# Recurrent attention and gMLP on one core: V sets, last-stage order, flag read and first weight load rearranged

## The chip, the core and the metric

The kernel runs on one core of a Trainium2 chip. TensorE (PE) multiplies, ScalarE (ACT) and VectorE (DVE) evacuate the accumulator banks (PSUM) and do the softmax and normalization, GpSimd (POOL) helps with small copies, and SyncE (SP) issues most DMAs. The metric is the device time of one execution in microseconds; a version is timed in several runs, and the median counts.

## The reference

Input: x of 2048 rows of 512, bf16. First a layernorm and an attention that is recurrent in its memory, 32 heads of 128, over 64 segments of 32 rows; then a gated MLP whose gate mixes all 2048 rows.

```python
def _A_ref(x, mem0, Wq, Wk, Wv, Wo, seg_len):     # x is the layernorm of the input
    mask = (idx[:, None] < M) | (idx[:, None] >= idx[None, :])   # M = 8 memory rows
    mem = mem0
    for s in range(n_seg):                          # 64
        xs = x[:, s * seg_len:(s + 1) * seg_len, :]
        h = jnp.concatenate([mem, xs], axis=1)      # 40 rows
        q, k, v = h Wq, h Wk, h Wv                  # per head
        p = softmax(where(mask, q k^T * scale, -1e9))
        o = einsum('bhte,hed->btd', p v, Wo)
        mem = o[:, :M, :]                           # feeds the next segment
        outs.append(o[:, M:, :])

def _B_ref(x, w_in, w_sp, b_sp, w_out):
    z = gelu(x w_in)                                # 512 -> 1792
    z1, z2 = z[..., :896], layernorm(z[..., 896:])
    g = einsum('ts,bsf->btf', w_sp, z2) + b_sp      # mixes all 2048 rows
    return einsum('bsf,fd->bsd', z1 * g, w_out)

h  = x + _A_ref(layernorm(x), ...)
h2 = h + _B_ref(layernorm(h), ...)
```

## The kernel before

All instructions come from lists that are written in order, one list for each engine; each engine runs its list in that order. An operation names what it reads and writes by tokens, and the emitter turns these into semaphore waits. Nothing reorders at run time, so where a matmul stands in the code of a segment is where PE runs it.

The work has four stages. In the start (to about 41.6 us) x, its normalization and the weights are loaded and the projections of the first chunk of 16 segments are made: `qkx_full` (L449) projects, for Q and K, "extra" rows of a chunk, eight of every segment's 32, head by head; `load_w(0, hq)` loads Wq in four pieces of eight heads, on the SP and ACT queues at once. Then come 64 segments one after the other, since each reads the memory rows that the one before made. A segment is QK (L539), scores (L590, L611) with the softmax on ACT, DVE and POOL, V (L645), PV (L670, and L676 for the extra rows), Wo (L708), and the memory rows (L735). PE would wait for the softmax and for the evacuation of PV; so PE gets filler matmuls there that later work needs: 16 matmuls from the list `gx` (L426, projections of the next chunk's extra rows), sets of four V matmuls for extra rows from the queue `gv` (L476), the output projection of the extra rows (`WoX_mm`, L764, with F matmuls L746 that collect a block's rows), and early gMLP projections (`zp_mm`, L836, 448 wide). `gv.pour(n)` takes up to n atoms of the queue, each with four matmuls, and stops at an atom that completes a bank, whose evacuation is then due. There are three places for it in a segment: ahead of PV, between PV and Wo, and behind Wo ("late"). With j4 = s % 4 and rb = s // 4, the pour ahead of PV happens where `rb == 0 or j4 < 3`; one between PV and Wo only if that one gave nothing.

PV writes four column groups c of 32 partitions; for each half b the four L676 matmuls come last, in the order c = 0, 1, 2, 3. Then ACT copies the groups c = 0 (each half apart) and c = 1 to `cT` (L694) and DVE c = 2 and c = 3 (L696). Wo reads the groups in the order 0, 2, 1, 3.

The last stage makes z2 (`z2_mm`, L1224: two groups of four matmuls of 448 columns a block) for the blocks from 10 to 15, while those from 0 to 9 were prepared within the segments; it normalizes z2 (`z2_norm`, `z2_apply` on DVE), makes z1 (`z1_group`, L1257, four matmuls of 512 columns) and mixes: out of each block of `order` five mix matmuls (L1264) go into five banks, with a lag of four blocks; the rest of the mixing and the output product (L1359) follow. Block 15 of the attention output is finished here too: an F group, 32 WoX matmuls, a scatter (L787), two adds on DVE, and its normalized rows, with those of block 14, are transposed by PE (L1333). The mixing weights come in slices by `load_wT` (L992) on SP.

A flag says whether the fast path may be used for these inputs; a small reduction and `check_flag` make it in mid-mixing. At the end each engine waits for it, reads it into a register (`reg_load`, L2073), SP waits for all DMAs, and each branches to the general path if it is set.

Of the kernel before, what the change touches and what calls it, by code (L numbers as in the profile page):

```python
# [169 lines left out]
def fast_path(nc, st, keep, A_x, A_mem0, A_Wq, A_Wk, A_Wv, A_Wo, A_seg_len, B_w_in, B_w_sp, B_b_sp, B_w_out, out):  # L170
# [8 lines left out]
    RB = S // 128  # L179
# [125 lines left out]
    def load_w(mi, hq, queues=("sp",)):  # L305
# [12 lines left out]
    for hq in range(4):  # L318
        load_w(0, hq, ("sp", "act"))
# [123 lines left out]
    def qkx_full(ck, i, bank):  # L443
        mi, h0 = i // 8, 4 * (i % 8)
        ws = (w_q, w_k)[mi]
        for hh in range(4):
            h = h0 + hh
            for dc in range(DC):
                pe(lambda e, h=h, dc=dc, hh=hh: e.matmul(ps[:, bank, hh * 128:(hh + 1) * 128], lhsT=ws[:, dc, h * DH:(h + 1) * DH],  # L449
                                                         rhs=hTe[:, ck, dc, :], start=(dc == 0), stop=(dc == DC - 1)),  # L450
                   reads=[("hTe", ck), ("W", mi, h // 8) if mi or dc < 2 else ("W", mi, h // 8, 1)], writes=[PB(bank)])
# [212 lines left out]
    def PV_half(s, b):  # L664
# [9 lines left out]
        for c in PVO[0]:  # L674
# [67 lines left out]
    def F_group(rb, bank, alone=False):  # L742
        sel, tok = (F2_sb, "F2") if alone else (F_sb, "F")
        for j in range(4):
            i = (4 * rb + j) % 8
            pe(lambda e, i=i, j=j: e.matmul(ps[32 * j:32 * j + 32, bank, :], lhsT=sel[:, :], rhs=part[:, i, :], start=True, stop=alone,  # L746
                                            tile_position=(0, 32 * j)),
               reads=[("part", i, 0), ("part", i, 1), tok] + ([("pm", rb % 2, g) for g in range(4)] if alone else []), writes=[PB(bank)])
# [11 lines left out]
    def WoX_mm(rb, qr, bgs=range(8)):  # L760
        for bg in bgs:
# [3 lines left out]
                                                           start=(i < 4), stop=(i >= H - 4), tile_position=(0, 32 * g)),  # L765
# [17 lines left out]

    def WoX_scatter(rb, bank, alone=False):
        for c in range(4):
            q = slice(32 * c, 32 * c + 32)
            pe(lambda e, q=q, c=c: e.matmul(ps[q, bank, :], lhsT=Sc[:, q], rhs=partx[:], start=alone, stop=True, tile_position=(0, 32 * c)),  # L787
               reads=["partx", "Sc"], writes=[PB(bank)])
# [217 lines left out]

    def wxp(rb, j4):
# [12 lines left out]
    for s in range(NSEG):  # L1020
# [104 lines left out]
        pv = gv.pour(1) if rb == 0 or j4 < 3 else []  # L1125
# [52 lines left out]
        if turn or (not pv and (s < 2 or s == 3 * CK + 1)):  # L1178
            late += [lambda f=f: f("act") for f in gv.pour(1)]
# [32 lines left out]
    def check_flag(bank):  # L1212
        pe(lambda e: e.matmul(ps[0:1, bank, 0:1], lhsT=okb[:, 0:1], rhs=onesrc[:, 0:1], start=True, stop=True),
# [20 lines left out]
    order = [NZP] + list(range(NZP)) + list(range(NZP + 1, RB))  # L1234
# [70 lines left out]
    sp(lambda e: e.dma_start(bsp_b, bass.AP(B_b_sp.tensor, B_b_sp.offset, [[0, 128], [1, S]])), writes=["bsp"], after=[lastK])  # L1305
    for i, rb in enumerate(order):
# [847 lines left out]
```

## Time and profile before

| what | value |
|---|---|
| runs | 843.51, 844.49 and 846.04 us; median 844.49 |
| profiled execution | 843.96 us, of which the span from the first to the last instruction is 842.1 |
| granted TensorE clock | 0.998 |
| busy: PE, ACT, DVE, POOL | 828.8, 513.3, 483.1, 145.5 us |
| attention ends, first mix, last matmul | 678.04, 693.27, about 837.65 us |

In the profile, a line number names the place in the code; a helper that makes many operations has one line. The chain of waits lists in order of time what ended last at each step: start, duration, engine and line. PEld is the weight load of a matmul, which overlaps the matmuls. A table by window gives, for each stretch of time, the busy time of PE, PEld, DVE, ACT and POOL with counts, then the granted clock, the busy share of the DMA engines and GB/s. A q behind an engine's name (SPq, ACTq) is its sequencer.

### The profile page before, as it was taken

The page shows a single profiled execution, that of the slowest core. Times are in us where ns is not written, and L with a number is a line of the kernel's source. Part 1 is how long each engine was busy: PE and PEld are TensorE (multiplying, and loading weights), DVE is VectorE, ACT ScalarE, POOL GpSimd, SP SyncE. Part 2 cuts the span into 40 slices and gives each one's busy share as a digit, 9 for nine tenths or more (in the row PEclk, how much of TensorE's full clock was granted, in tenths as well). Part 3 has the DMA queues.
Part 4 walks back from the last instruction along what each step waited for, and adds up shares of the span by engine and source line. Part 5 has one row for each costly group of instructions (what it writes and reads, how often), then busy time and mean ns, then how long its engine had stood idle before and what let it go on. Part 6 is the DMA issues. An engine that isn't in the chain of part 4 may idle for free.

```text
span 842.1 us, 48381 instructions
## 1 busy us (share of the span) xinstructions
PE 828.8 (98%) x21968; PEld 479.7 (57%) x21974; DVE 483.1 (57%) x1224; ACT 513.3 (61%) x1547; POOL 145.5 (17%) x413
## 2 busy tenths in 40 slices
PE   8999999999999999999999999999999999999997
PEld 8665555555565555555655556555556544444443
DVE  4546565656565666665656656565556576554343
ACT  3466777777777777777777777777667676300000
POOL 5212111111211111121112111211111123100000
PEclk9999999999999999999999999999999999999999
DMA  9982222221222222221212222433334289022101
GB/s 329 386 228 75 73 61 60 60 60 56 63 73 55 67 56 65 68 70 54 74 48 66 59 56 70 102 90 89 77 83 89 65 278 287 1 101 92 53 12 47
DMA packets 106180, 80.01 MB, mean 95 GB/s; under 512 B 48552, under 2 KB 95536, under 8 KB 105968
## 3 DMA queue, kind: packets, MB, share of 16 engines
q1 hardware_dynamic: 104048, 74.03, 30.0%
q8 instruction: 174, 2.85, 1.5%
q10 hardware_dynamic: 1648, 2.49, 0.9%
q14 instruction: 38, 0.31, 0.1%
q0 software_dynamic: 272, 0.33, 0.1%
HBM read 43.72 MB, written 22.87 MB: 79 GB/s over the span
## 4 chain that ended last, share of the span: by engine, by line
PE 95%; DMA 2%; ACT 1%; SPq 1%; issue 1%; DVE 1%; ACTq 0%; POOL 0%; DVEq 0%
PE f_ps L539 27%; PE f_ps L708 14%; PE f_ps L645 13%; PE f_ps L1264 12%; PE f_ps L426 4%; PE f_ps L764 4%; PE f_ps L476 3%; PE f_ps L1359 3%; PE f_ps L670 3%; PE f_ps L449 2%; PE f_ps L836 2%; PE f_ps L1257 2%; PE f_ps L590 2%; PE f_ps L611 1%; PE f_ps L1224 1%; DMA f_arena<-in_A_Wq_dram 1%
## 5 line engine op out<-in xcount | busy, mean ns | idle before, releaser
L539 PE MATMUL f_ps<-f_arena,f_hT 128*32 128x512 bf16 (+1 forms) x5120 | 241.7, 337 | 0.3
L539 PEld LDWEIGHTS f_ps<-f_arena,f_hT 128*32 128x32 bf16 x5120 | 117.5, 96 | 99.3 <-ACT f_hT L738 33.8
L550 ACT ACTIVATE f_Tst<-f_ps 128x512 bf16<-128x512 f32 (+2 forms) x320 | 146.8, 511 | 35.1 <-PE f_ps L539 34.3
L645 PE MATMUL f_ps<-f_arena,f_hT 128*32 128x512 bf16 x2048 | 139.1, 379 | 0.0
L708 PE MATMUL f_ps<-f_arena,f_cT 128*32 128x256 bf16 x4096 | 131.0, 273 | 0.4 <-ACT f_cT L694 0.2
L635 POOL TENSOR_TENSOR f_E_sb<-f_R_sb,f_E_sb 128x64 bf16<-128x64 f32 x128 | 47.4, 370 | 407.5 <-ACT f_R_sb L627 406.9
L708 PEld LDWEIGHTS f_ps<-f_arena,f_cT 128*32 128x32 bf16 x4096 | 97.9, 96 | 24.4 <-ACT f_cT L694 8.5
L558 DVE STREAM_TRANSPOSE f_QT<-f_Tst 128x256 uint32<-128x256 uint32 x128 | 57.1, 446 | 84.3 <-ACT f_Tst L550 79.7
L657 DVE TENSOR_SCALAR f_V_sb<-f_ps 128x512 bf16<-128x512 f32 (+1 forms) x128 | 71.4, 558 | 54.2 <-PE f_ps L645 54.2
L1264 PE MATMUL f_ps<-f_arena 128*128 128x512 bf16 x448 | 100.6, 379 | 1.0 <-DMA f_arena<-wT_d 1.0
L1264 PEld LDWEIGHTS f_ps<-f_arena 128*128 128x128 bf16 x448 | 43.7, 98 | 53.5 <-DMA f_arena<-wT_d 1.1
L696 DVE TENSOR_SCALAR f_cT<-f_ps 128x256 bf16<-128x256 f32 x128 | 48.4, 420 | 40.6 <-PE f_ps L676 40.6
L604 ACT ACTIVATE f_E_sb<-f_ps 128x224 bf16<-128x224 f32 x128 | 45.4, 355 | 39.0 <-PE f_ps L616 38.0
L694 ACT ACTIVATE f_cT<-f_ps 128x160 bf16<-128x160 f32 (+1 forms) x192 | 51.5, 328 | 25.4 <-PE f_ps L676 25.1
L558 DVE STREAM_TRANSPOSE f_KT<-f_Tst 128x256 uint32<-128x256 uint32 (+2 forms) x192 | 60.8, 342 | 5.7 <-ACT f_Tst L550 3.0
L727 ACT ACTIVATE f_part<-f_ps 128x256 bf16<-128x256 f32 x128 | 49.2, 384 | 19.9 <-PE f_ps L708 14.3
L645 PEld LDWEIGHTS f_ps<-f_arena,f_hT 128*32 128x32 bf16 x2048 | 46.4, 95 | 20.1 <-issue 0.3
L738 ACT ACTIVATE f_hT<-f_ps 128x16 bf16<-128x16 f32 x126 | 23.2, 184 | 46.6 <-PE f_ps L735 46.6
L1270 DVE TENSOR_TENSOR f_arena<-f_ps,f_arena 128x512 f32<-128x512 f32 x28 | 19.3, 690 | 52.7 <-PE f_ps L1264 52.7
L576 DVE CAST f_ps<-f_mask 128x224 f32<-128x224 bf16 x80 | 29.8, 373 | 28.6 <-ACT f_hT L406 25.7
L627 ACT ACTIVATE f_R_sb<-f_R_sb 128x160 f32<-128x160 f32 x128 | 43.1, 337 | 4.4 <-ACT f_Vs L488 0.4
L426 PE MATMUL f_ps<-f_arena,f_hTe 128*32 128x512 bf16 x640 | 41.5, 379 | 0.0
(131 smaller groups left out, 1154.7 us busy)
## 6 DMA issues: line engine op xcount, KB each, us to landing
wT_d<-f_wst SPq DMA_DIRECT2D x64, 128.0 KB, 1.7
f_arena<-wT_d SPq DMA_DIRECT2D x32, 256.0 KB
f_arena<-in_A_Wv_dram SPq DMA_DIRECT2D x4, 1024.0 KB
f_arena<-in_A_Wk_dram SPq DMA_DIRECT2D x4, 1024.0 KB
f_arena<-in_A_Wo_dram SPq DMA_DIRECT2D x4, 1024.0 KB
f_Vx<-vext_d SPq DMA_DIRECT2D x62, 64.0 KB
vext_d<-f_Vs SPq DMA_DIRECT2D x22, 128.0 KB, 2.9
zp_d<-f_Vs SPq DMA_DIRECT2D x20, 112.0 KB
```

The costliest lines, as they stand in the source:

```text
L426: pe(lambda e, c=c, rhs=rhs: e.matmul(ps[32 * c:32 * c + 32, bank, :], lhsT=hTe[:, ck, dc, 32 * sg:32 * sg + 32], rhs=rhs, start=(dc == 0) ...
L539: pe(lambda e, dc=dc, c=c, rhs=rhs: e.matmul(ps[32 * c:32 * c + 32, bank, 0:32 * nh], lhsT=hT[:, sl, dc, :], rhs=rhs, start=(dc == 0), sto ...
L550: act(lambda e: e.activation(out=st_.rearrange("p (hp i r) -> p hp i r", i=32, r=2), in_=ps[:, bank, 0:64 * np_].rearrange("p (hp r i) -> ...
L558: dve(lambda e: e.transpose(out=dst, in_=src), reads=tok, writes=[(nm, b, k) for k in halves(b, p0, np_)])
L635: pool(lambda e: e.tensor_tensor(out=ev, in0=rv, in1=ev, op=ALU.mult), reads=[("R", b), ("Ex", b)], writes=[("Ex", b)])
L645: pe(lambda e, dc=dc, c=c, c0=c0: e.matmul(ps[32 * c:32 * c + 32, bank, 0:w], lhsT=hT[:, sl, dc, :], rhs=w_v[:, dc, c0:c0 + w], start=(dc ...
L657: dve(lambda e: e.tensor_scalar(out=dst, in0=src, scalar1=VSC, scalar2=None, op0=ALU.mult), reads=[PB(bank)], writes=tok)
L694: act(lambda e: e.activation(out=dst, in_=src, func=ACT.Copy, scale=UNSC), reads=[PB(bank)], writes=tok)
L696: dve(lambda e: e.tensor_scalar(out=dst, in0=src, scalar1=UNSC, scalar2=None, op0=ALU.mult), reads=[PB(bank)], writes=tok)
L708: pe(lambda e, h=h, g=g, i=i, b=b, c=c: e.matmul(ps[32 * g:32 * g + 32, bank, 0:d1 - d0], lhsT=cTh[:, i, 8:40], rhs=w_o[:, h, d0:d1], star ...
L727: act(lambda e: e.activation(out=part[:, s % 8, d0:d1], in_=ps[:, bank, 0:d1 - d0], func=ACT.Copy), reads=[PB(bank)], writes=[("part", s % ...
L1264: pe(lambda e: e.matmul(ps[:, bank, 0:TB], lhsT=z2[:, sc, fb * 128:(fb + 1) * 128], rhs=wTb[tb % 2][:, :, sc, :], start=first, stop=last), ...
```

## The change

Five edits. (1) The first piece of Wq is split: heads 0 to 3 alone, then heads 4 to 7, each on both queues; the first projection group waits for the first part alone. (2) The L676 matmuls of PV's second half come in the order c = 2, 1, 3, 0. (3) The V set ahead of PV is poured by `v_ahead`: in the first and the last block of four segments, and else only at j4 = 0 and 1 (1 and 2 in block 12); what is not poured there comes between PV and Wo, and the late pour also happens in segment 2. (4) In the last stage block 15's attention output is finished first; the order of z2 blocks is a list in which 11 comes third and 12 and 13 come later; block 15's scatter is one matmul with 128 columns; blocks 14 and 15 are stored and read back by a transposing DMA instead of by PE; the second slice set of mixing weights, w_out and h are loaded behind that. (5) The flag is read at the start of the third of four parts of mixing, where SP also waits for all DMAs issued until then; at the end SP waits for those issued since.

```diff
-    def load_w(mi, hq, queues=("sp",)):
+    def load_w(mi, hq, queues=("sp",), u=None):
         parts = len(queues)
         n = DC // parts
         wd, ws = ((A_Wq, w_q), (A_Wk, w_k), (A_Wv, w_v))[mi]
         wr = wd.rearrange("(dc p) h e -> p dc (h e)", p=128)
-        cols = slice(hq * 8 * DH, (hq + 1) * 8 * DH)
+        cols = slice(hq * 8 * DH, (hq + 1) * 8 * DH) if u is None else slice(4 * u * DH, 4 * (u + 1) * DH)
         for k in range(parts):
-            tok = ("W", mi, hq) if k == 0 else ("W", mi, hq, k)
+            tok = ("Wh", k) if u == 0 else ("W", mi, hq) if k == 0 else ("W", mi, hq, k)
             em.add(queues[k], lambda e, k=k: e.dma_start(ws[:, k * n:(k + 1) * n, cols], wr[:, k * n:(k + 1) * n, cols]), dma=True, writes=[tok])
             em.mark_const(tok)
 
     load_xe(0, 0)
     load_xe(1, 1, "act")
     for hq in range(4):
-        load_w(0, hq, ("sp", "act"))
+        for u in (None,) if hq else (0, 1):
+            load_w(0, hq, ("sp", "act"), u)
         if hq == 1:
             act(lambda e: e.preload_act_table_set("natural_log_exp_and_others"))
     load_x(0, 4)
...
-                   reads=[("hTe", ck), ("W", mi, h // 8) if mi or dc < 2 else ("W", mi, h // 8, 1)], writes=[PB(bank)])
+                   reads=[("hTe", ck), ("Wh", dc // 2) if i == 0 else ("W", mi, h // 8) if mi or dc < 2 else ("W", mi, h // 8, 1)], writes=[PB(bank)])
...
-        for c in PVO[0]:
+        for c in (PVO[0], (2, 1, 3, 0))[b]:
...
         for bg in bgs:
             b, g = bg // 4, bg % 4
             h = 16 * b + 4 * qr + g
             pe(lambda e, h=h, g=g, i=8 * qr + bg: e.matmul(ps[32 * g:32 * g + 32, WXB, :], lhsT=cTx[:, rb % 2, i, :], rhs=w_o[:, h, :],
-                                                           start=(i < 4), stop=(i >= H - 4), tile_position=(0, 32 * g)),
+                                                           start=(i // 8 == first and i % 8 < 4), stop=(i // 8 == last and i % 8 >= 4), tile_position=(0, 32 * g)),
                reads=[("cTx", rb % 2, qr), ("Wo", h // 8)], writes=[PB(WXB)])
     def WoX_range(rb, i0, i1):
...
+    def v_ahead(rb, j4):
+        return rb in (0, RB - 1) or j4 in ((1, 2) if rb == 12 else (0, 1))
-        pv = gv.pour(1) if rb == 0 or j4 < 3 else []
+        pv = gv.pour(1) if v_ahead(rb, j4) else []
-        if turn or (not pv and (s < 2 or s == 3 * CK + 1)):
+        if turn or (not pv and (s < 3 or s == 3 * CK + 1)):
...
-        pe(lambda e: e.matmul(ps[0:1, bank, 0:1], lhsT=okb[:, 0:1], rhs=onesrc[:, 0:1], start=True, stop=True),
+        pe(lambda e: e.matmul(ps[:, bank, 0:1], lhsT=onesrc[:, 0:128], rhs=okb[:, 0:1], start=True, stop=True),
-    def xn_copy(rb, j, bank):
-        src = psb[:, bank, 0:512].rearrange("p (dc c) -> p dc c", dc=DC)
-        dve(lambda e: e.tensor_copy(out=xT2(rb), in_=src), reads=[PB(bank)], writes=[("xn2T", rb)], after=[lastop["s"], lastop["x"]])
-    order = [NZP] + list(range(NZP)) + list(range(NZP + 1, RB))
+    order = [10, 0, 11, 1, 2, 3, 4, 5, 6, 12, 7, 13, 8, 9, 14, 15]
...
     sp(lambda e: e.dma_start(bsp_b, bass.AP(B_b_sp.tensor, B_b_sp.offset, [[0, 128], [1, S]])), writes=["bsp"], after=[lastK])
+    for qr in (1, 2, 3, 0):
+        WoX_mm(RB - 1, qr, first=1, last=0)
+    F_group(RB - 1, XB, False)
+    F_add(RB - 1, XB)
+    endA = em.by_eng["pe"][-1]
+    WoX_evac(RB - 1)
     for i, rb in enumerate(order):
         if rb >= NZP:
             z2_mm(rb, 0, zbank())
             z2_mm(rb, 1, zbank())
-        if i == 0:
-            F_group(RB - 1, XB)
-            for qr in range(4):
-                WoX_mm(RB - 1, qr)
-            endA = em.by_eng["pe"][-1]
-            WoX_evac(RB - 1)
-            load_wT(1, [endA])
-            sp(lambda e: e.dma_start(w_out, B_w_out.rearrange("(fb p) d -> p fb d", p=128)), writes=["w_out"], after=[endA])
         z1_next()
         if rb < NZP:
             z2_gelu(rb)
         if i < 12:
             z1_next()
         if i == 1:
-            WoX_scatter(RB - 1, XB)
-            h_done(RB - 1, XB)
+            pe(lambda e: e.matmul(ps[:, CB, :], lhsT=Sc[:], rhs=partx[:], start=True, stop=True),
+               reads=["partx", "Sc"], writes=[PB(CB)])
+            h_done(RB - 1, CB)
+        if i in (1, 2):
+            xn2_apply(RB - 3 + i, i % 2)
+            xn2_store(RB - 3 + i, i % 2)
+        if i == 2:
+            for r in range(RB - 2, RB):
+                xn2T_dma(r, [lastop["s"], lastop["x"]])
+            load_wT(1, [endA])
+            sp(lambda e: e.dma_start(w_out, B_w_out.rearrange("(fb p) d -> p fb d", p=128)), writes=["w_out"], after=[endA])
             for r in range(RB):
                 sp(lambda e, r=r: e.dma_start(h_sb[:, r, :], h_d[r]), reads=[("hd", r)], writes=[("hs", r)], after=[lastQ])
-        if i in (1, 2):
-            xn2_apply(RB - 3 + i, i % 2)
-        if i in (3, 4):
-            r, j, bank = RB - 5 + i, i % 2, zbank()
-            for dc in range(DC):
-                pe(lambda e, dc=dc, j=j, bank=bank: e.transpose(out=psb[:, bank, dc * 128:(dc + 1) * 128], in_=xo[:, j, dc * 128:(dc + 1) * 128],
-                                                                identity=ident[:, :]), reads=[("xo", j), "ident"], writes=[PB(bank)])
-            xn_copy(r, j, bank)
         z2_norm(rb)
         if i > 0:
             z2_apply(order[i - 1])
...
+    def get_flag(e, eng):
+        flags[eng] = e.alloc_register("flag_" + eng)
+        return e.reg_load(flags[eng], flag[:])
...
+        if tb == 2:
+            for eng in Emitter.ENGS:
+                em.add(eng, lambda e, eng=eng: get_flag(e, eng), reads=["flag"])
+            em.add("sp", None, after=em.final_dma_ops())
-    for eng in Emitter.ENGS:
-        em.add(eng, None, reads=["flag"])
+    em.add("sp", None, after=em.final_dma_ops())
-    return em, sems, dma_sems, flag
+    return em, sems, dma_sems
...
+    flags = {}
-            em, sems, dsems, flag = fast_path(nc, st, keep, *args)
+            em, sems, dsems = fast_path(nc, st, keep, flags, *args)
-            r = e.alloc_register("flag_" + name)
-            e.reg_load(r, flag[:])
-            if name == "sp":
-                for d in done:
-                    e.wait_ge(dsems[d.dma_sem], d.dma_val)
-            with e.If(e.snap(r) != 0):
+            with e.If(e.snap(flags[name]) != 0):
```

On PE, in segment 14 (j4 = 2), from V's last matmul to the first of PV's second half (V L645, fillers L426, V set L476, PV L670 and L676). Before:

```order
L645 MATMUL f_ps<-f_arena,f_hT 32x512 [waits fdma9]
L426 MATMUL f_ps<-f_arena,f_hTe 32x512 x16
L476 MATMUL f_ps<-f_arena,f_hTe 32x512 x4
L670 MATMUL f_ps<-f_E_sb,f_V_sb 128x40 [waits fs_dve]
L670 MATMUL f_ps<-f_E_sb,f_V_sb 128x40 [waits fs_act]
L670 MATMUL f_ps<-f_E_sb,f_V_sb 128x40 x14
L676 MATMUL f_ps<-f_E_sb,f_Vx 128x4x16 [waits fs_pool]
L676 MATMUL f_ps<-f_E_sb,f_Vx 128x4x16 x3
```

And now, with all line numbers higher by one:

```order
L646 MATMUL f_ps<-f_arena,f_hT 32x512 [waits fdma12]
L427 MATMUL f_ps<-f_arena,f_hTe 32x512 x16
L671 MATMUL f_ps<-f_E_sb,f_V_sb 128x40 [waits fs_dve]
L671 MATMUL f_ps<-f_E_sb,f_V_sb 128x40 [waits fs_act]
L671 MATMUL f_ps<-f_E_sb,f_V_sb 128x40 x14
L677 MATMUL f_ps<-f_E_sb,f_Vx 128x4x16 [waits fs_pool]
L677 MATMUL f_ps<-f_E_sb,f_Vx 128x4x16 x3
```

The row of four V matmuls is gone from this place.

On PE, at the end of the attention and the start of the last stage (F matmuls L746, z2 L1224, WoX L764, z1 L1257). Before:

```order
L746 MATMUL f_ps<-f_part,f_F_sb 32x512 [waits fs_dve]
L746 MATMUL f_ps<-f_part,f_F_sb 32x512 x3
L1224 MATMUL f_ps<-f_arena,f_hTe 128x448 [waits fdma0,fs_act]
L1224 MATMUL f_ps<-f_arena,f_hTe 128x448 x7
L746 MATMUL f_ps<-f_part,f_F_sb 32x512 [waits fs_dve]
L746 MATMUL f_ps<-f_part,f_F_sb 32x512 x2
L746 MATMUL f_ps<-f_part,f_F_sb 32x512 [waits fs_act]
L764 MATMUL f_ps<-f_arena,f_cTx 32x512 [waits fs_pool]
L764 MATMUL f_ps<-f_arena,f_cTx 32x512 x31
L1257 MATMUL f_ps<-f_arena 128x512 [waits fdma32,fs_act]
L1257 MATMUL f_ps<-f_arena 128x512 x3
```

And now (F L747, WoX L765, z2 L1218, z1 L1251, the scatter L1316):

```order
L747 MATMUL f_ps<-f_part,f_F_sb 32x512 [waits fs_dve]
L747 MATMUL f_ps<-f_part,f_F_sb 32x512 x3
L765 MATMUL f_ps<-f_arena,f_cTx 32x512 [waits fs_act]
L765 MATMUL f_ps<-f_arena,f_cTx 32x512 x23
L765 MATMUL f_ps<-f_arena,f_cTx 32x512 [waits fs_pool]
L765 MATMUL f_ps<-f_arena,f_cTx 32x512 x7
L747 MATMUL f_ps<-f_part,f_F_sb 32x512 [waits fs_dve]
L747 MATMUL f_ps<-f_part,f_F_sb 32x512 x2
L747 MATMUL f_ps<-f_part,f_F_sb 32x512 [waits fs_act]
L1218 MATMUL f_ps<-f_arena,f_hTe 128x448 [waits fdma2]
L1218 MATMUL f_ps<-f_arena,f_hTe 128x448 x7
L1251 MATMUL f_ps<-f_arena 128x512 [waits fdma34,fs_act]
```

The WoX matmuls come ahead of the z2 pair of block 10. A few rows later, still ahead of the first mix (L1258), stands the z2 pair of block 11, behind the scatter:

```order
L1251 MATMUL f_ps<-f_arena 128x512 x3
L1316 MATMUL f_ps<-f_partx,f_Sc 128x512 [waits fs_dve]
L1218 MATMUL f_ps<-f_arena,f_hTe 128x448 [waits fdma12,fs_act]
L1218 MATMUL f_ps<-f_arena,f_hTe 128x448 x3
L1218 MATMUL f_ps<-f_arena,f_hTe 128x448 [waits fs_act]
L1218 MATMUL f_ps<-f_arena,f_hTe 128x448 x3
L1251 MATMUL f_ps<-f_arena 128x512 [waits fs_act]
```

On SP, behind the last of the first slice set of mixing weights: transposing loads (L829, now L824) of normalized blocks, the bias, the second slice set of mixing weights (L992, now L987). Before:

```order
L829 DMA_TRANSPOSE f_arena<-xn_d 128x4x128 [waits fdma19]
L829 DMA_TRANSPOSE f_arena<-xn_d 128x4x128
L1305 DMA f_arena<-in_B_b_sp_dram 128x2048
L992 DMA f_arena<-wT_d 128x1024 [waits fs_pe]
L992 DMA f_arena<-wT_d 128x1024
L992 DMA f_arena<-wT_d 128x1024 [waits fdma24]
L992 DMA f_arena<-wT_d 128x1024 x5
L1317 DMA f_arena<-in_B_w_out_dram 128x7x512
L798 DMA h_d<-f_hbuf 128x512 [waits fs_dve]
```

And now, with the stores L801 of blocks 14 and 15 and their transposing loads:

```order
L824 DMA_TRANSPOSE f_arena<-xn_d 128x4x128 x2
L1299 DMA f_arena<-in_B_b_sp_dram 128x2048
L793 DMA h_d<-f_hbuf 128x512 [waits fs_dve]
L801 DMA xn_d<-f_xo 128x512 [waits fs_dve]
L801 DMA xn_d<-f_xo 128x512 [waits fdma26,fs_dve]
L824 DMA_TRANSPOSE f_arena<-xn_d 128x4x128 [waits fdma25]
L824 DMA_TRANSPOSE f_arena<-xn_d 128x4x128 [waits fdma26]
L987 DMA f_arena<-wT_d 128x1024 x6
L987 DMA f_arena<-wT_d 128x1024 [waits fdma35]
L987 DMA f_arena<-wT_d 128x1024
L1326 DMA f_arena<-in_B_w_out_dram 128x7x512 [waits fdma1]
```

The second slice set stands behind two stores and two transposing loads more, and behind block 15's store L793.

More of the change, by code (lines that the diff above doesn't have):

```diff
@@ L740, in mem_out, with F_group @@
             reads=[PB(GB)], writes=[("hTm", s + 1, hf)])
-    def F_group(rb, bank, alone=False):
-        sel, tok = (F2_sb, "F2") if alone else (F_sb, "F")
+    def F_group(rb, bank, joint):
+        sel, tok = (F2_sb, "F2") if joint else (F_sb, "F")
         for j in range(4):
             i = (4 * rb + j) % 8
-            pe(lambda e, i=i, j=j: e.matmul(ps[32 * j:32 * j + 32, bank, :], lhsT=sel[:, :], rhs=part[:, i, :], start=True, stop=alone,
+            pe(lambda e, i=i, j=j: e.matmul(ps[32 * j:32 * j + 32, bank, :], lhsT=sel[:, :], rhs=part[:, i, :], start=True, stop=True,
                                             tile_position=(0, 32 * j)),
-               reads=[("part", i, 0), ("part", i, 1), tok] + ([("pm", rb % 2, g) for g in range(4)] if alone else []), writes=[PB(bank)])
+               reads=[("part", i, 0), ("part", i, 1), tok] + ([("pm", rb % 2, g) for g in range(4)] if joint else []), writes=[PB(bank)])
     def F_add(rb, bank):
@@ L758, in load_h, with WoX_mm @@
         sp(lambda e: e.dma_start(hbuf[:, rb % 2, :], xr[:, rb, :]), writes=[("h", rb % 2)], after=behind())
-    def WoX_mm(rb, qr, bgs=range(8)):
+    def WoX_mm(rb, qr, bgs=range(8), first=0, last=3):
         for bg in bgs:
@@ L782, in WoX_evac @@
         dve(lambda e: e.tensor_copy(out=partx[:], in_=ps[:, WXB, :]), reads=[PB(WXB)], writes=["partx"])
[L784 to L788, printed above, removed]
     def h_done(rb, bank):
```

2 lines of the change are left out of this document (1 added, 1 removed).

## The prediction

> **What bounds the kernel now.** I read the page first (busy rows, chain by engine), then the chain of waits over the whole run and inside each stage, then tables of busy time by window.
>
> ```profile
> PE 828.8 (98%) x21968; PEld 479.7 (57%) x21974; DVE 483.1 (57%) x1224; ACT 513.3 (61%) x1547; POOL 145.5 (17%) x413
> PE 95%; DMA 2%; ACT 1%; SPq 1%; issue 1%; DVE 1%; ACTq 0%; POOL 0%; DVEq 0%
> ```
>
> TensorE (PE) is busy for 98% of the span and carries 95% of the chain; 842.1 - 828.8 leaves 13 us in which it does nothing. So an edit can win in three ways only: matmuls that leave the chain, matmuls that move into a PE wait, or one of the few stretches without PE made shorter. Those stretches are the first 9 us, the border between attention and last stage, and the tail.
>
> **Part 1, the V sets.** A segment lasts from one QK block (L539) to the next. Segments 14 and 15, and 23, in the chain and in the table by window:
>
> ```profile
> 184.88 3.11 PE f_ps L539 x72
> ...
> 191.04 0.22 PE f_ps L476 x3
> 191.26 0.20 PE f_ps L670 x16
> 191.46 0.04 PE f_ps L676 x4
> 191.50 0.12 PE f_ps L670 x16
> 191.62 0.04 PE f_ps L676 x3
> ...
> 200.94 0.21 PE f_ps L670 x16
> 201.15 0.04 PE f_ps L676 x4
> 201.18 0.17 PE f_ps L670 x16
> 201.35 0.10 PE f_ps L676 x4
> 201.45 0.55 PE f_ps L476 x8
> ```
>
> ```profile
> 184.88:194.78 9.90, 9.90 (x338) 5.97 (x332) 5.90 (x16) 7.72 (x24) 1.93 (x5) 1.00 0.22 64
> 194.78:204.52 9.74, 9.74 (x322) 5.74 (x316) 5.83 (x16) 7.44 (x23) 1.38 (x4) 1.00 0.19 55
> 273.68:283.60 9.92, 9.92 (x320) 6.01 (x316) 6.52 (x17) 7.44 (x23) 1.37 (x4) 1.00 0.23 64
> ```
>
> Segment 14 has 16 ordinary fillers (L426, the rows left out) and one V set of four (L476; one record is missing) ahead of PV (L670, L676); segment 15 has the 16 alone there, and eight V matmuls between PV and Wo. The four cost 9.90 - 9.74 = 0.16 us and not their 0.22, since with 16 fillers PV itself takes 0.52 (0.21+0.04+0.17+0.10) against 0.40. The eight between PV and Wo stand in every segment that has work for them, and segment 15 is the shortest kind in spite of them: they fill the time in which ScalarE and VectorE evacuate PV, so I price them at nothing. Segment 23 has four V matmuls behind Wo instead, beside the F matmuls, and lasts 9.92: 0.18 more than segment 15.
>
> By the new rule the pre-PV set leaves segments 6, 10, 14, 18, 22, 26, 30, 34 and 38 (nine) and comes to 40, 41 and 44 (three): -6 x 0.16 = -0.96. In 7 and 23 the four behind Wo move ahead of Wo: -2 x 0.18 = -0.36. Segment 2 gets four behind its own post slot: +0.18. Segments 3, 39 and 43 get sets between PV and Wo, at nothing by the reading above; if that cover were gone each would cost at most 0.2. The 448-wide projection sets of 54, 58 and 63 shift by one set each way, counted as nothing. Sum of part 1: -1.14, with 0.3 to either side.
>
> **Part 2, the last stage.** The chain at the border, the wait at its end, and later z2 blocks:
>
> ```profile
> 686.70 6.52 DMA f_arena<-wT_d
> ...
> 693.27 1.25 PE f_ps L1264 x5
> ...
> 711.36 1.51 PE f_ps L1224 x8
> ```
>
> ```profile
> PE f_ps L1264 <- DMA f_arena<-wT_d: 1.0, 1, 1.0
> ```
>
> ```profile
> L1333 PE MATMUL f_ps<-f_ident,f_xo 128*128 128x128 bf16 x8 | 0.8, 220 | 0.0
> ```
>
> ```profile
> 678.04:693.27 15.23, 13.87 (x102) 5.80 (x97) 10.75 (x25) 11.86 (x19) 4.37 (x11) 1.00 0.84 283
> 693.27:757.00 63.73, 63.68 (x300) 29.32 (x302) 38.08 (x77) 20.56 (x34) 12.16 (x26) 1.00 0.43 136
> ```
>
> The first mix (L1264) starts when the last slice of the spatial weights lands, at 693.23 (686.70 + 6.52), after PE had waited 1.0 us for it; PE was ready at 692.2. From then on PE has no gap: 63.68 of 63.73 busy. So what leaves the time behind 693.27 is won in full, and what is added ahead of it is free as far as the wait reaches. The change takes the z2 pair of block 11 (L1224, 1.51) from behind to ahead. The eight PE transposes of blocks 14 and 15 (L1333, 0.8 busy), which stand ahead, are dropped for a store and a transposing DMA; the F matmuls, the 32 WoX matmuls and the scatter stay ahead in another order. PE is then ready at 692.2 + 1.5 - 0.8 = 692.9, still before the weights, since SP's queue up to their last slice is unchanged. The wait that remains, 0.3, is the cover; without it each 0.1 more ahead costs 0.1. Gain: -1.5. The DMA path of blocks 14 and 15 takes some 7 us more than the transposes did if it is as slow as the weights' 6.52, so about 700; the last z1 groups that read it run at about 710. The second weight block, now behind it on SP, is read only in the second part of the mixing, past 750.
>
> **Part 3, the end.**
>
> ```profile
> 837.67 0.42 DVE f_xo L1366
> ```
>
> ```profile
> 838.13 0.37 ACTq L1368 DMA_DIRECT2D out_dram<-f_xo  x1
> ```
>
> ```profile
> L2073 PEldq TENSOR_LOAD <-f_flag x1: 490/490/490, 835.4 to 835.4; - x1
> ...
> L2073 ACTq TENSOR_LOAD <-f_flag x1: 490/490/490, 838.5 to 838.5; - x1
> ```
>
> ```profile
> L2077 ACTq COMPARE_BRANCH  x1: 58/58/58, 839.1 to 839.1; - x1
> ```
>
> ```profile
> L2082 SPq DRAIN  x1: 49/49/49, 841.3 to 841.3; - x1
> L2082 DVEq DRAIN  x1: 57/57/57, 841.3 to 841.3; - x1
> L2082 ACTq DRAIN  x1: 80/80/80, 841.8 to 841.8; - x1
> ```
>
> After its output DMA, issued at 838.13 behind the last add, ACT loads the flag (0.49), branches at 839.1, and reaches the closing drain at 841.8, last of all. Without the load it comes 0.5 earlier, at 841.3, level with SP and DVE, which shorten too. Gain -0.5; at least 0 if another engine holds the end, at most -0.8. The load now sits in the middle of mixing; PE's sequencer runs ahead of its array there (it loaded the flag at 835.4, over 2 us before the add of its last matmuls at 837.67), so it costs nothing; without that cover it costs 0.5.
>
> **Part 4, the start.**
>
> ```profile
> 1.56 7.06 DMA f_arena<-in_A_Wq_dram
> ...
> 8.75 1.34 PE f_ps L449 x16
> ```
>
> ```profile
> PE f_ps L449 <- DMA f_arena<-in_A_Wq_dram: 1.1, 1, 1.1
> ```
>
> ```profile
> 28.00:53.00 25.00, 23.92 (x520) 15.45 (x516) 10.53 (x24) 11.87 (x30) 5.87 (x12) 1.00 1.06 358
> ```
>
> ```profile
> L928 SPq DMA_DIRECT2D f_arena<-in_A_Wo_dram x4: 640/3132/6159, 30.0 to 40.4; - x4
> ```
>
> ```profile
> DMA packets 1934, 3.87 MB, mean 387 GB/s; under 512 B 63, under 2 KB 63, under 8 KB 1931
> DMA packets 1370, 1.41 MB, mean 353 GB/s; under 512 B 21, under 2 KB 1367, under 8 KB 1367
> ```
>
> The first weight group waits 1.1 us for Wq; with half of it loaded first it may start up to that much earlier; I take 0.9 as the most. But the DMA engines are full from there to 53 us (share 1.06), and segment 0's Wo matmuls wait for the last quarter of Wo, issued at 40.4 into that full queue. PE work ahead of that is not the limit: bytes are. The last two rows are the same queue at 18 to 28 us with 2 KB packets and at 46 to 50 with 1 KB packets. The change cuts the first 1 MB from 2 KB rows to 1 KB rows: 1.05 MB/353 - 1.05 MB/387 = 0.26 us more. So I count +0.26 and not -0.9. The Trainium skill (DMA: Bandwidth & Descriptors, Specifications) gives 512 bytes as the least transfer for line rate; by that the cut would cost 0 and this term would be 0, which the 353 against 387 here does not bear out.
>
> **Part 5, the PV order.** From the page's groups:
>
> ```profile
> L708 PE MATMUL f_ps<-f_arena,f_cT 128*32 128x256 bf16 x4096 | 131.0, 273 | 0.4 <-ACT f_cT L694 0.2
> ...
> L708 PEld LDWEIGHTS f_ps<-f_arena,f_cT 128*32 128x32 bf16 x4096 | 97.9, 96 | 24.4 <-ACT f_cT L694 8.5
> ```
>
> The four L676 matmuls of a half signal one after the other: the row 201.35 has four in 0.10, three steps of 0.034. In the second half c=2 now comes first, so VectorE's copy of c=2 (the third Wo group's input) starts 0.07 earlier, and ScalarE's copy for c=0, the first group's second half, 0.10 later. The Wo matmuls (L708) waited 0.4 us in all, over 64 segments, though their weight loads waited for ACT's copies 8.5; so both copies come just in time, and a shift of 0.07 one way and 0.10 the other nets out small. The bounds are -0.4 (all of that wait gone) and +6.3 (63 segments with the full 0.10), the second a rival below. I take +0.1, near the lower end since the row's 0.4 lies there, and slower since the delay is the larger shift; the range, without the rival, takes +0.8, an eighth of 6.3.
>
> **Sum.** -1.14 - 1.5 - 0.5 + 0.26 + 0.1 = -2.8. The profiled execution took 843.96 (span 842.1 and 1.86 around it), 0.53 under the median of the runs (844.49). By its own time 841.2, by the median 841.7; between the two I predict 841.4. A measurement of this kernel tells about 0.3% (2.5 us) from no change, so faster means under 842.0.
>
> **Rivals.**
> - *The new order of PV delays Wo* (slower). c=0's second half is read in the first Wo group; if its ScalarE copy ends last there, each of 63 segments loses the whole 0.10: 63 x 0.10 = +6.3, less the 0.1 already in the sum: 847.6. It decides from the point where the copy has less than 0.10 of slack. For it: in the page the weight load of L708 waits for ACT's cT (8.5 us). Against: PE itself waited only 0.4, and eight matmuls stand between PV and Wo. The Trainium skill (TensorE: Matmul & The Clock Gate, The cost: per-tile semaphore tail) has increments of tiles serialize at 26.3 ns each; the trace bears out the queueing, with 34 here. Chance 0.07.
> - *The border gives nothing* (same). If the weights land later, or the z2 evacuations of block 11 hold the three rotating banks so that PE is 1.5 later at its first mix, part 2 falls to 0: 842.9. For it: PE has only 0.3 in hand. Against: ACT is busy 11.86 of 15.23. Chance 0.2.
> - *The start gain survives* (faster). If the last quarter of Wo is not what segment 0 ends on, the 0.26 goes and up to 0.9 comes: 841.4 - 0.26 - 0.9 = 840.2. Against it stands the share of 1.06. Chance 0.13.
> - *The end or the flag read fails*: SP's waits or the code fetch hold the end, or PE stalls 0.5 in mid stream: 841.4 + 0.5 = 841.9, or 842.4 with both. Chance 0.15.
> - *My forecast*, 840.6 to 842.0: 0.45.
>
> **Numbers.** Faster: forecast 0.40 of its 0.45, the start 0.13, 0.05 of the end's, 0.02 of the border's: 0.60. Slower by over 2.5: PV order, 0.07. Same: the rest, 0.33. The range is 839.9 to 843.3: below, the start rival's 840.2 less the 0.3 of part 1; above, the border rival's 842.9 and 0.4 for the outer half of the PV bound. It leaves out the PV rival (0.07) and what lies beyond the single bounds (about 0.12).
>
> **What would show it.** Segments 14 and 15 both 9.74, and 23 too (part 1 right). The first mix within 0.2 of the weights' landing, PE's wait there 0.1 to 0.6, and the time from first mix to last matmul 1.5 shorter (part 2). ACT's drain 0.5 after the last add less than now (part 3). First L449 at 7.8 but the end of segment 0 unmoved or 0.3 later (part 4); if it is 0.9 earlier I was wrong on the limit. Wo groups in segment 16 within 0.02 of before (part 5). I would be wrong if 20-filler segments were 0.1 longer, or if PE came to the first mix after the weights had landed.

## The result, and the profile after

| | runs | median us | range us |
|---|---|---|---|
| before | 6 | 845.78 | 843.51 to 848.33 |
| changed | 6 | 841.70 | 841.21 to 843.30 |

The ratio is 0.9959, with a 95% interval of 0.9943 to 0.9974: 4.1 us less. A second set of runs (e5 below) gave 841.23 against 845.16, ratio 0.9941 (0.9919 to 0.9964). The forecast time, 841.4, was 0.3 away from 841.7, and that is partly luck: the three runs of before that the prediction had seen (median 844.49) lay 1.3 below the six, and the gain that it summed up (2.8) was 1.3 too small, so the two misses cancel.

The page of the changed kernel, busy time and chain by engine:

```profile
PE 828.1 (99%) x21956; PEld 480.4 (57%) x21963; DVE 482.0 (57%) x1221; ACT 516.1 (61%) x1549; POOL 145.4 (17%) x413
PE 94%; DMA 3%; SPq 1%; DVE 1%; issue 0%; ACT 0%
```

The span fell from 842.1 to 840.3, by 1.8 alone, though the median fell by 4.1. Stage by stage, from the same instructions in each trace (first score matmul of segment 1, last Wo matmul, first mix, last matmul, end of span; us):

| execution | segment 1 | last Wo | first mix | last matmul | end |
|---|---|---|---|---|---|
| before | 58.00 | 678.04 | 693.27 | 837.63 | 842.11 |
| changed | 61.89 | 679.31 | 693.70 | 836.36 | 840.29 |
| difference of the stage | +3.89 | -2.62 | -0.84 | -1.70 | -0.55 |

So this execution lost 3.9 in the start, where the forecast had 0.26, and won 5.7 behind it. The chain of waits shows the loss:

```profile
2.75 10.34 DMA f_arena<-in_A_Wq_dram
13.09 0.05 issue
13.13 10.89 PE f_ps L450 x192
...
42.26 12.67 DMA f_arena<-in_A_Wo_dram
54.93 0.04 issue
54.97 2.35 PE f_ps L709 x43
```

```profile
PE f_ps L709 <- DMA f_arena<-in_A_Wo_dram: 1.4, 1, 1.4
```

A second table by window, ahead of and behind this wait; the third column from the end is the granted clock:

```profile
50.00:54.00 4.00, 3.09 (x82) 1.43 (x79) 1.54 (x5) 2.54 (x9) 1.83 (x5) 1.00 0.90 297
55.00:58.40 3.40, 3.40 (x68) 2.39 (x72) 0.48 (x1) 0.95 (x3) 0.00 (x0) 0.53 0.49 123
```

The last quarter of Wo landed at 54.93, 2.3 later than before (52.64, by the DMA's semaphore in the trace); PE waited 1.4 us for it; and then it ran at about half the clock for 3.4 us, which cost some 1.6 more. That is the part of the result that the experiments had to explain.

The rest answers to the prediction's rows. Segments 14 to 16, and 23, in the chain:

```profile
187.72 3.11 PE f_ps L540 x72
...
193.87 0.21 PE f_ps L671 x16
194.08 0.04 PE f_ps L677 x4
194.11 0.17 PE f_ps L671 x16
194.28 0.10 PE f_ps L677 x4
...
197.46 3.11 PE f_ps L540 x72
...
207.20 3.11 PE f_ps L540 x72
...
217.09 3.11 PE f_ps L540 x72
...
276.14 3.11 PE f_ps L540 x72
...
285.88 3.11 PE f_ps L540 x72
```

Segments 14, 15 and 23 last 9.74 each (before: 9.90, 9.74, 9.92); segment 14's V set is gone from the place ahead of PV. Segment 16, which keeps it, lasts 9.89. At the border and at the end:

```profile
693.70 1.24 PE f_ps L1258 x5
```

```profile
836.40 0.42 DVE f_xo L1359
```

```profile
PE f_ps L1258 <- DVE f_st L1233: 0.2, 1, 0.2
```

```profile
L2073 ACTq COMPARE_BRANCH  x1: 58/58/58, 837.3 to 837.3; - x1
```

```profile
L2078 ACTq DRAIN  x1: 80/80/80, 840.0 to 840.0; - x1
```

From first mix to last add 142.70, before 144.40. ACT branches 0.9 after the last add begins (837.3 - 836.4) instead of 1.4 (839.1 - 837.67), and still needs 2.7 from there to its drain.

### The profile page after: what moved, and what is told of

Same layout as the page of the kernel before. It is cut to its first block, busy times and chain, and to the rows that moved or that the text cites. A ratio compares the mean times of both kernels' runs of the same rounds, so it can differ in the third digit from the quotient of the medians.

```text
span 840.3 us, 48359 instructions
## 1 busy us (share of the span) xinstructions
PE 828.1 (99%) x21956; PEld 480.4 (57%) x21963; DVE 482.0 (57%) x1221; ACT 516.1 (61%) x1549; POOL 145.4 (17%) x413
## 4 chain that ended last, share of the span: by engine, by line
PE 94%; DMA 3%; SPq 1%; DVE 1%; issue 0%; ACT 0%
PE f_ps L540 27%; PE f_ps L709 14%; PE f_ps L646 13%; PE f_ps L1258 12%; PE f_ps L427 4%; PE f_ps L765 4%; PE f_ps L477 3%; PE f_ps L1352 3%; PE f_ps L671 3%; PE f_ps L1251 2%; PE f_ps L831 2%; DMA f_arena<-in_A_Wo_dram 2%; PE f_ps L591 1%; PE f_ps L450 1%; DMA f_arena<-in_A_Wq_dram 1%; SPq L923 1%
## 5 line engine op out<-in xcount | busy, mean ns | idle before, releaser
L1258 PE MATMUL f_ps<-f_arena 128*128 128x512 bf16 x448 | 100.5, 379 | 0.2 <-DVE f_st L1233 0.2
L1258 PEld LDWEIGHTS f_ps<-f_arena 128*128 128x128 bf16 x448 | 43.7, 98 | 53.2 <-DVE f_st L1233 0.7
L695 ACT ACTIVATE f_cT<-f_ps 128x160 bf16<-128x160 f32 (+1 forms) x192 | 55.4, 329 | 24.5 <-PE f_ps L677 23.7
```

The lines of the kernel that those rows point to most:

```text
L695: act(lambda e: e.activation(out=dst, in_=src, func=ACT.Copy, scale=UNSC), reads=[PB(bank)], writes=tok)
L1258: pe(lambda e: e.matmul(ps[:, bank, 0:TB], lhsT=z2[:, sc, fb * 128:(fb + 1) * 128], rhs=wTb[tb % 2][:, :, sc, :], start=first, stop=last), ...
```

## The experiments

**e1: the split undone.** The first piece of Wq comes whole again:

```diff
-        for u in (None,) if hq else (0, 1):
-            load_w(0, hq, ("sp", "act"), u)
+        load_w(0, hq, ("sp", "act"))
```

> The changed kernel with the first piece of Wq loaded whole again (two DMAs of 512 KB); all else as changed. In the profiled execution of the changed kernel segment 0 ends 3.9 us later than before (scores of segment 1 start at 61.89, before 58.00). Theory A, the split causes it: the scores of segment 1 start near 58.0 again and the whole is 3 to 4 us faster than the changed kernel, about 838, ratio to before about 0.991. Rival B, an accident of that execution, with the split worth the forecast 0.26: segment 1 still starts at 60 to 62 or the whole stays within 1 us of 841.7, ratio about 0.996.

**e2: the split alone, in the kernel before** (the same lines the other way round).

> The kernel before with the split of Wq's first piece alone. Theory A: segment 1's scores start near 61.9, not 58.0, PE waits over 1 us for the last quarter of Wo, and the time is 3 to 4 us over that of before, ratio 1.004 to 1.005. Rival B: 0.3 us slower, ratio 1.000. Rival C, the start gain survives: 0.9 faster, 0.999.

**e3: as many DMAs, but with 2 KB rows.** For the split piece:

```diff
-        cols = ... slice(4 * u * DH, 4 * (u + 1) * DH)
+        cols = slice(hq * 8 * DH, (hq + 1) * 8 * DH)
+            d0, d1 = (k * n, (k + 1) * n) if u is None else (k * n + u, k * n + u + 1)
```

> The changed kernel, but the first piece of Wq is split into its DMAs by 128-row parts instead of by heads: as many DMAs on each queue, each with 2 KB rows instead of 1 KB; the first group then waits for all of it. If the row size is what delays the queue (1 KB packets), the delay goes: the last quarter of Wo lands near 52.6 and the time is 3 to 4 us under the changed kernel, like the version without the split. If the additional DMA issues do it (two more on SP's queue, 0.5 to 0.6 us each, with everything behind them later), the last quarter still lands past 54 and the time stays near 841.7.

**e4: matmuls of no use into the wait**, in segment 0, ahead of the first Wo matmul that reads the last quarter:

```diff
+                if keepwarm and c == 2 and bg == 4:
+                    for _ in range(keepwarm):
+                        pe(lambda e: e.matmul(ps[:, XB, 0:160], lhsT=onesrc[:, 0:128], rhs=onesrc[:, :], start=True, stop=True), ...
```

> The changed kernel with 20 matmuls of no use (160 columns, the start's warming ones, into a free bank) in segment 0, between the Wo matmuls that the third and the last quarter of Wo feed. In the changed kernel PE waited 1.44 us there and then ran at a granted clock of 0.5 to 0.6 for about 3.5 us. Theory: that slow clock is half of the delay and comes from the wait; with PE kept busy the clock stays at 1.0 and the time is 1.5 us under the changed kernel (about 840.2). Rival: the clock has another cause, the time stays at 841.7 or rises by up to 1.3.

Measured, all on one chip, median of before 845.47:

| version | median us | ratio to before (95%) | segment 1 in its profile |
|---|---|---|---|
| e1, no split | 842.29 | 0.9971 (0.9956 to 0.9987) | 59.01 |
| e2, split alone | 846.42 | 1.0004 (0.9990 to 1.0017) | 60.55 |
| e3, 2 KB rows | 841.98 | 0.9964 (0.9950 to 0.9977) | 59.29 |
| e4, 20 matmuls | 846.34 | 1.0012 (0.9995 to 1.0029) | 64.44 |

Theory A fell in its size: without the split the median was not 838, and the split alone cost between -0.8 and +1.4 us, not 3 to 4. Rival C, 0.9 faster, lies just outside of that interval too. e3 was not 3 to 4 us faster either: 2 KB rows changed nothing that the timings show, and its last quarter of Wo landed at 53.92, not near 52.6. The profiles still pointed the other way (the split executions start segment 1 later), which is why the changed kernel was run again. e4 failed as made: its matmuls waited themselves, for a bank that DVE had not released:

```profile
PE f_ps L711 <- DVE f_Vs L491: 2.1, 1, 2.1
```

```profile
54.90:60.00 5.10, 5.10 (x68) 4.24 (x72) 0.00 (x0) 0.38 (x1) 0.00 (x0) 0.50 0.42 109
```

But it showed the slow clock a second time behind a long wait: 2.1 us idle, then 0.50 for the 5 us shown.

**e5: the changed kernel again; e6: all four pieces of Wq split; e7: e4 with a bank that is free.** e6 and e7 against the changed kernel:

```diff
-        for u in (None,) if hq else (0, 1):
+        for u in (0, 1):
...
-                        pe(lambda e: e.matmul(ps[:, XB, 0:160], ...
+                        pe(lambda e: e.matmul(ps[:, CB, 0:160], ...
```

> The changed kernel itself, on the chip of the two runs that follow. Segment 1's scores started at 61.89 in its profiled execution and at 59.0 and 59.3 in the two versions without a split by heads. If the split costs 2 to 3 us in every execution, segment 1 starts past 60.5 here too and the ratio to before is about 0.996. If that was one execution's accident, it may start anywhere from 58 to 62 and the ratio is 0.994 to 0.996.

> The changed kernel with all four pieces of Wq split by heads, not the first alone: four times the 1 KB packets and eight more DMA issues instead of two. Theory A (the split delays everything behind it on the queues, 1 to 3 us): the last quarter of Wo lands 4 us or more later than with one split, segment 1 starts past 63, and the time is 3 us or more over e5_changed_again. Forecast's price, 0.26 for each MB of 1 KB packets: 0.8 over e5. Rival (it is hidden, or an accident): within 0.5 of e5.

> As e4_warm, but the 20 matmuls of no use write a bank that was already released (that of PV's first column group, second half), so that they wait for nothing; in e4_warm they waited 2.1 us for another bank and PE then ran at a granted clock of 0.5 for 6 us. Theory (the clock falls where PE idles over 1 us): no granted clock below 1.0 in 53 to 60 us, and a time of 0 to 1.5 us under e5_changed_again, by how often the wait of over 1 us comes in an execution. Rival: the clock falls all the same, or the 20 matmuls cost their 1.3 us.

| version | median us | ratio to before (95%) | segment 1 in its profile |
|---|---|---|---|
| e5, changed | 841.23 | 0.9941 (0.9919 to 0.9964) | 59.34 |
| e6, four splits | 842.35 | 0.9963 (0.9948 to 0.9979) | 60.53 |
| e7, 20 matmuls | 843.11 | 0.9972 (0.9957 to 0.9987) | 60.22 |

In e5's profile the wait for Wo was short, and the clock held (chain, wait, and table by window):

```profile
1.55 7.21 DMA f_arena<-in_A_Wq_dram
8.77 0.14 issue
8.90 1.86 PE f_ps L450 x16
```

```profile
PE f_ps L709 <- DMA f_arena<-in_A_Wo_dram: 0.3, 1, 0.3
```

```profile
53.00:60.00 7.00, 6.73 (x204) 4.05 (x200) 3.35 (x10) 5.04 (x16) 0.32 (x2) 1.00 0.56 163
```

Segment 1 starts at 59.34 here, 2.5 earlier than in the first profile of the same kernel, so much of that 3.9 differs from execution to execution. Not all of it does: the traces of the versions, those of e8 to e10 below included, agree that the split itself delays the loads (the landing is read from the DMA's semaphore, the wait is PE's ahead of the Wo matmul that reads the last quarter):

| execution | first piece of Wq | GB/s, 3 to 9 us | last quarter of Wo lands | PE waits for it | segment 1 |
|---|---|---|---|---|---|
| before | whole | 372 | 52.64 | no | 58.00 |
| e1 | whole | 340 | 53.04 | no | 59.01 |
| e3 | by rows, 2 KB | 295 | 53.92 | 0.4 | 59.29 |
| e5 | by heads, 1 KB | 319 | 53.98 | 0.3 | 59.34 |
| e2 | by heads | 300 | 54.06 | 0.5 | 60.55 |
| e9 | by heads | 303 | 54.16 | no | 59.52 |
| changed | by heads | 301 | 54.93 | 1.4 | 61.89 |
| e6 | all four by heads | 312 | 55.17 | 0.4 | 60.53 |
| e10 | by heads | 303 | 55.31 | 1.6 | 60.67 |
| e8 | by heads | 297 | 55.33 | 1.7 | 62.29 |

The rates are the last number of these rows (before, e3, e5):

```profile
3.00:9.00 6.00, 3.92 (x38) 3.43 (x36) 2.46 (x6) 1.59 (x2) 2.98 (x10) 1.00 1.03 372
```

```profile
3.00:9.00 6.00, 3.64 (x36) 3.11 (x34) 2.46 (x6) 1.88 (x2) 3.15 (x11) 0.93 0.95 295
```

```profile
3.00:9.00 6.00, 3.46 (x35) 3.09 (x33) 2.46 (x6) 1.88 (x2) 2.98 (x10) 0.95 0.98 319
```

Every split execution moves fewer bytes in 3 to 9 us and gets the last quarter of Wo 0.9 to 2.7 us later than the two with a whole piece; e1, e2 and e3 ran on one chip. Two executions with a whole piece are few, but none of the eight others overlaps them. The rows of e3 are 2 KB, and it stands with the others; this points to the greater number of smaller DMAs, not to the row size, as far as one execution of e3 goes. How much of the delay reaches the end of an execution on average stays open: the timings allow no more than the 1.4 of e2's interval, and e1 against the changed kernel shows no gain from leaving the split out. Four splits instead of one cost 1.1 by the medians (not clear of zero by the ratios), near the 0.8 that the forecast's price gives and far from theory A's 3. e7 kept the clock at 1.00 through 53 to 60:

```profile
53.00:60.00 7.00, 7.00 (x180) 4.63 (x176) 2.26 (x7) 3.89 (x13) 0.24 (x1) 1.00 0.61 156
```

but its median was 1.9 above e5's, so its rival on the price held: in its trace the last quarter landed at 53.90 and the matmul that reads it started at 54.90, behind the 20. Long waits for Wo are still no exception: three of the six profiled executions with the one split and no extra matmuls had one of 1.4 us or more. e7's own execution had no long wait to cover, so it does not show that a busy PE keeps the clock.

**e8, e9, e10: the order of PV, the V rule, and the flag read undone**, each in the changed kernel, one run each:

```diff
-        for c in (PVO[0], (2, 1, 3, 0))[b]:
+        for c in PVO[0]:
...
-        pv = gv.pour(1) if v_ahead(rb, j4) else []
+        pv = gv.pour(1) if rb == 0 or j4 < 3 else []
...
-        if tb == 2:
-            for eng in Emitter.ENGS:
-                em.add(eng, lambda e, eng=eng: get_flag(e, eng), reads=["flag"])
+    for eng in Emitter.ENGS:                      # behind the last output
+        em.add(eng, lambda e, eng=eng: get_flag(e, eng), reads=["flag"])
```

> The changed kernel with the old order of the four extra-row matmuls of PV's second half (0, 1, 2, 3). One look, read by segments without a stall. In the changed kernel a segment with 20 fillers ahead of PV lasts 9.893 and one with 16 lasts 9.742; before they lasted 9.900 and 9.740. If the order made these differences, they return to 9.900 and 9.740; the forecast said the new order costs 0.015 in the first kind, so that here 9.885 would be seen. If other code made them (the first mix of places), 9.893 and 9.742 stay.

> The changed kernel with the old rule for the V sets (segments 6 to 38 at j4 = 2 get a pre-PV set again, 40, 41 and 44 none; segment 2 no late one; the projection sets of 54, 58 and 63 as before). One look. Segments 10, 14, 18, 22, 26, 34 and 38 last 9.89 instead of 9.742, segment 40 lasts 9.742 instead of 9.893, segment 23 lasts 9.91. At the border: the first mix came 14.0 to 14.5 us after the last Wo matmul in the changed kernel and 15.0 to 15.2 before. If the last projection set of segment 63, which the new rule moves ahead, is what lets SP issue the weights 0.8 earlier, the border is about 14.8 here; if the last stage's own new order does it, it stays at 14.0 to 14.5.

> The changed kernel with the flag read at the end again and the check matmul with one row and one column again. One look. From the last matmul to the end 4.48 us as before (3.93 to 4.2 in the changed kernel), and first mix to last matmul 142.83 instead of 142.66, since the one-row check matmul took 0.17 more at its place. If something else in the change shortened the end, 3.9 to 4.2 stays.

e8 took 842.42, e9 841.24, e10 841.83, beside 842.36 for before in its one run there; single runs differ by more than these effects, so only the traces are read. e8, segment 16, and e9, segment 14, by their QK blocks in the chain:

```profile
207.91 3.11 PE f_ps L540 x72
217.81 3.11 PE f_ps L540 x72
```

```profile
186.26 3.11 PE f_ps L540 x72
196.15 3.11 PE f_ps L540 x72
```

With the old order of PV a segment with 20 fillers lasts 9.90 again (median 9.901 over its stall-free ones, 9.893 with the new order), and one with 16 lasts 9.740 (9.742). The new order wins 0.007 in the first kind; the forecast had a loss of 0.015. With the old V rule segment 14 lasts 9.89 and segment 23 9.906: the rule alone makes part 1. (Segment 40, which should have come back to 9.742, lasts 9.82.) e9's border is 678.71 to 692.69, 13.98, as short as in the changed kernel, so it is not the projection set moved by the rule that shortens it. With the split, the PV order or the flag read undone it stays at 13.98, 14.07 and 14.44, and in e2, with the old last stage, it is 15.00: that leaves the last stage's own rearrangement. In e10 first mix to last matmul is 142.84, 0.18 longer, and ACT branches late again:

```profile
L2071 ACTq COMPARE_BRANCH  x1: 58/58/58, 836.0 to 836.0; - x1
```

```profile
L2076 ACTq DRAIN  x1: 81/81/81, 839.6 to 839.6; - x1
```

That is 1.6 after the last matmul (834.44), in the changed kernel 0.9, before 1.5; the wait behind the branch was 3.6 here, against 2.7, so its end at 5.5 behind the last matmul misses the 4.48 that I expected. None of the versions is faster than the changed kernel by more than the noise.

## Why the prediction was right, and where it was not

*Part 1, the V sets: right in the rule, and in every price but one.* Nine segments lost 0.158 each, 40 and 41 gained 0.15 each, 7 and 23 lost 0.17 each, and segment 2 gained 0.18. Segment 44, which the forecast charged with 0.16 too, gained nothing: it got its set and lasts 9.921, before 9.923. In before, PE waited there in the middle of PV for POOL, as the chain shows, and the set fills that wait:

```profile
487.81 0.32 POOL f_E_sb L635
488.13 0.05 issue
488.18 0.21 PE f_ps L676 x4
```

So the sum is about -1.3 by the stall-free segments, where the forecast had -1.14; e9 gives it back in the segments that have no stall there. The sets between PV and Wo were free: 39 lasts 9.744 with eight V matmuls there, 9.736 before with four. Of the -2.62 of this stage about 1.1 is left when the PV order (part 5) is counted too. It lies in stalls that sit in other segments in each execution, and no run shows that the change removed any.

*Part 2, the last stage: right in its mechanism, too small.* Block 11's z2 pair left the time behind the first mix: z2 took 7.57 us there before and 6.06 now, the -1.51 of the sum. Two things came on top. The check matmul with one output row, which I had not priced, had cost 0.17: from the fourth matmul ahead of it to the fourth behind it, start to start, it takes 1.71 in before, e2 and e10, and 1.54 in the nine executions with the new one. And one step of the working failed: the forecast held the landing of the weights at 693.23 "since SP's queue up to their last slice is unchanged". From the last Wo matmul to the first mix it took 14.39 instead of 15.23, and between 13.98 and 14.54 in all ten executions with the new last stage. Table by window, e5, from the last Wo matmul on:

```profile
677.66:691.64 13.98, 13.93 (x98) 6.38 (x90) 10.68 (x23) 10.89 (x19) 4.34 (x10) 1.00 0.84 292
```

PE is busy for 13.93 of 13.98 with z2 of block 11 already in it; before it was busy for 13.87 of 15.23. The last slice landed 15.18 behind the last Wo matmul in before and 14.96 in e2, but 13.66 to 14.45 in the ten. Mostly SP issued it earlier: the issue ended 9.4 behind that matmul in before, 8.8 in the changed kernel, 8.6 in e1 and 8.1 in e9. SP's list up to there is the same, but it has waits for other engines in it, and which of them the rearrangement shortened was not tried. PE was ready sooner, too, than the 14.9 that I added up. In part that is because the transposes had cost not 0.8 but 1.4 with the waits around them: PE spent 689.22 to 692.31 on them and on two z1 groups of 0.86 each. The cover of 0.3 that the forecast counted on is gone in some executions. Its sign of being wrong, PE coming to the first mix after the weights, showed in e1 and e9, where they landed at 13.72 and 13.66 and PE came at 13.98. What is late in the profiled execution of the changed kernel is DVE, by 0.2.

*Part 3, the end: right.* From the last matmul to the end it took 4.47 in before and 4.52 in e2, and 3.93 to 4.22 in the nine executions with the early flag read. e10 brings the late branch back, though its end is 1.0 longer than before, through the wait behind the branch. The flag read in mid-mixing cost PE nothing: the mixing span is 142.66 to 142.67 in all versions with it.

*Part 4, the start: right that the 0.9 would not be won, and not borne out in its price and its reason.* The first group does start earlier in some split executions (7.65 in e8, before 8.75; 8.90 in e5 and 8.95 in e9), and in none of them is segment 1 earlier, which fits the reading that bytes and not PE work are the limit. But the working has PE wait for the last quarter of Wo in before, and there it does not: that quarter landed at 52.64 and the matmul that reads it started at 52.68. The term is 1 KB rows against 2 KB rows, 0.26; in the traces the delay is 0.9 us at least, and e3 has it with 2 KB rows. So the rate of 353 against 387 in two different stretches, from which the 0.26 comes, did not price this split. The timings do not contradict the size: e2's interval, -0.8 to +1.4, holds the 0.26 and e6 fits 0.8 for three more. The rival of a surviving gain of 0.9 is just outside. The Trainium skill's 512 bytes (DMA: Bandwidth & Descriptors, Specifications) would give 0; between 0 and 0.26 no timing here decides. What the forecast did not foresee is that the end of segment 0 differs between executions by up to 4 us, through the wait for Wo and the clock behind it.

*Part 5, the PV order: wrong in sign, too small to matter.* -0.007 in 19 segments with 20 fillers, about as much in those with projection sets, +0.002 in the others: -0.2 in all, where I had +0.1. The rival of 6.3 did not come.

Together: -1.3 (V), -0.2 (PV), -0.8 (border), -1.7 (mixing), -0.5 (end) is -4.5. The timings say -4.1 and -3.9, with intervals of 2.6 us and more, so the difference of 0.4 to 0.6 says nothing sure about the start. The forecast's -2.8, with +0.26 for the start in it, missed 0.8 at the border, 0.2 at the check matmul, 0.3 at PV and 0.2 in the V sets.

## What to carry to other kernels

Price a moved group of instructions by the stage it leaves and the wait it fills, with rows of two otherwise equal stages; that held to 0.01 us in 14 of the 15 segments priced here. The fifteenth had a wait of its own at the place, which its row of the chain would have shown. What a DMA queue "unchanged" will do is not known from its list: each wait in it can move. And one profile is one execution: a stage in which transfers decide must be seen in several before its difference is a property of the change, and traces taken for another question count too.

## What the runs showed of the hardware

A PE wait of over 1 us can cost more than itself, but its length alone does not decide that. Behind a wait of 0.3 (e5) the granted clock stayed at 1.00, also behind 0.5 for Wo and 1.0 us of idle time in e2:

```profile
PE f_ps L736 <- issue: 1.0, 1, 1.0
```

```profile
54.00:60.00 6.00, 4.92 (x132) 2.88 (x136) 1.41 (x3) 3.03 (x9) 0.00 (x0) 1.00 0.73 104
```

Behind 1.4 (changed), 1.7 (e8) and 2.1 (e4) it fell to about 0.5; and behind the 1.1 that the first group waits for Wq in before, it stood at 0.56 (rows of e8 and of before):

```profile
55.70:59.00 3.30, 3.30 (x68) 2.20 (x64) 0.18 (x1) 0.95 (x3) 0.00 (x0) 0.50 0.48 124
```

```profile
9.00:12.00 3.00, 3.00 (x35) 3.00 (x33) 0.89 (x2) 0.60 (x1) 2.08 (x10) 0.56 1.05 391
```

But behind 1.6 in e10 it stayed at 1.00:

```profile
PE f_ps L709 <- DMA f_arena<-in_A_Wo_dram: 1.6, 1, 1.6
```

```profile
55.40:60.00 4.60, 4.60 (x128) 2.65 (x132) 1.29 (x3) 2.94 (x8) 0.00 (x0) 1.00 0.56 158
```

In the clock records of the traces a slow stretch lasts 3.41 us (before, 9.36 to 12.77; changed, 55.21 to 58.62; e8, 55.63 to 59.04) or twice that (e4, 54.01 to 60.84). At half the clock 3.41 us cost about 1.7, which is the 1.6 of the first profile. The equal lengths look as if the clock were set anew at fixed steps of time, so that it would matter where in a step a wait falls; that is an inference from these records, and no run tested it. That the clock falls after some of these waits is what the rows show; that the idle time causes it was tested by no pair of runs that differ in nothing else.
